# Softmax denominators from the third batch element on: VectorE turns and sums the exponentials in place of TensorE's multiplication by ones

## The chip, the cores and the metric

The kernel runs on one core of a Trainium2 chip. The metric is the time of one execution on the device in microseconds (us), lower is better. TensorE is written PE, VectorE DVE, ScalarE ACT, GpSimd POOL; SP is the engine whose queue issues most of the transfers.

## The reference

Eight batch elements, 12 heads, 448 positions, head size 64. Attention with normalised q and k, then a mixer over tokens (448 to 256 to 448) and over channels (768 to 1536 to 768), all in float32.

```python
q_n, k_n = rmsnorm(q, g_q), rmsnorm(k, g_k)            # (8, 12, 448, 64)
scores = matmul(q_n, k_n.T) / sqrt(64)
attn = exp(scores - max);  attn = attn / (sum(attn, over keys) + 1e-9)
x = matmul(attn, v)                                     # put together to (8, 448, 768)
h = max(x.T @ w_tok1, 0) @ w_tok2;   u = x + h.T
out = u + max(u @ w_ch1, 0) @ w_ch2
```

## The kernel before

Every instruction's place is set by the program: each engine runs its instructions in the order in which the code emits them (`manual_schedule`), and an instruction that waits holds up everything behind it on its engine. Lists of work items with costs are merged into one list (`merge`, `place`), and that order is the order on all engines.

Heads are taken in pairs `p` (0 to 47, six to a batch element) and pairs in steps of two, `t` (0 to 23, three to an element). While the mixer of element b runs, the attention of element b + 1 runs between its matmuls. The work of step t:

- `turn_qk`: from pair 12 on DVE turns q and k by 32x32 blocks (L436) and ACT scales q (L439).
- `score(t, k)` for seven groups k of 64 keys: four 64x64 matmuls (L459) make scores with keys on the partitions. They fill two of the four PSUM buffers of `ps_S`; ACT writes the exponentials (L463) to the tile `e`.
- `values`: four matmuls with v for each k add up the output (`o_ps`, L532).
- `group_sums(t, k)`: DVE adds the seven `e` tiles into `es` (L500). `es` is one buffer, 128x896: two pairs, 64 sums per head on the partitions.
- `row_sums(t)`: four matmuls with a matrix of ones (`one_c`, L512) add the 64 partitions of each head. The result `d_ps` takes the two other buffers of `ps_S`, and every partition of a head holds the denominator.
- `denominators`: for each pair DVE turns `d_ps` out of PSUM (`dt`, L561), takes reciprocals (`rc`, L563), turns them back spread over 32 columns (`rd`, L575) and multiplies `o_ps` into `uT` (L578).

From step t = 9 (`BIG`) a step is two blocks on PE: the first holds scores 0 and 1 of step t, the rest of `values` of step t - 1, `row_sums(t - 1)` and score 2; the second holds scores 3 to 6 and four of `values`. Six to eight units of the mixer stand between blocks (`BLOCKS`). Steps 6 to 8 are cut into four smaller parts by `att_step`.

The mixer's matmuls write `m_ps`, of which there are two buffers. In the first half of the channel mixer (`ch1`, L1102) a group of six matmuls fills one buffer, and DVE (L1108) or ACT (L1112, L1124) takes it out; seven such groups belong together (`PRODUCTS`, a form of Strassen's scheme). In the second half (`ch2`, L1168) eight matmuls fill a buffer, and DVE (L1183) or ACT (L1179) takes it out. X forms (L1142) are sums for ch2 on DVE and POOL.

Of the kernel before, what the change touches and what calls it, by code (L numbers as in the profile page):

```python
# [8 lines left out]
F32 = mybir.dt.float32  # L9
# [74 lines left out]
def whole(ctx, tc, shifted, pre, q, k, v, g_q, g_k, moe_w_tok1, moe_w_tok2, moe_w_ch1, moe_w_ch2, out):  # L84
# [454 lines left out]

    def row_sums(t):  # L540
        es = st.pop(("es", t))
        for p in (2 * t, 2 * t + 1):
            st["d", p] = s_tile("d_ps")
            ones(p, es[:, p % 2, :], start=True, stop=True)

    def denominators(ps):

        def begin(p):
            b, j = divmod(p, NPAIR)
            if j == 0:  # L550
                st["uT", b] = uT_pool.tile([P, NC, S], F32, name="uT")
# [9 lines left out]
            nc.vector.transpose(out=dt[:], in_=src)  # L561
            st["rc", p] = rc = pre.nt_pool.tile([P, NB], F32, name="rc")
            nc.vector.reciprocal(out=rc[:], in_=dt[:].rearrange("p (n c) -> p n c", c=32)[:, :, 0])  # L563

        def raw(p):

            b, j = divmod(p, NPAIR)
# [4 lines left out]
        def end(p):  # L572
            b, j = divmod(p, NPAIR)
            rd = rd_pool.tile([P, S], F32, name="rd", tag="rd")
            nc.vector.transpose(  # L575
                out=rd[:].rearrange("p (n c) -> p n c", c=32),
                in_=st.pop(("rc", p))[:].unsqueeze(2).to_broadcast([P, NB, 32]))
# [10 lines left out]
    def big_step(t, second):  # L588
# [6 lines left out]
        def first_block():  # L595
            if live:
                score(t, 0)
                score(t, 1)
            if more and t > BIG:
                pre.reduce(n, st)  # L600
                pre.square(n + 1, st)
            for k in range(NK - 2 - (t > BIG), NK):
                values(last, k)
            row_sums(t - 1)
            for i in last:
                st.pop(("v", i))
            if live:
                score(t, 2)
# [11 lines left out]
        if not second:  # L620
# [7 lines left out]
            between += roots[:1] + ends[:2] + roots[1:2]  # L628
            between += [it for both in zip(ends[2:], roots[2:4]) for it in both] if more else ends[2:]
# [5 lines left out]
        between += [item(group_sums, t, k) for k in (5, 6)] + loads(n + 3)  # L635
# [24 lines left out]
    def att_step(g):  # L660
# [8 lines left out]
        def finish():  # L669
# [7 lines left out]
            if s == 0 and t:  # L677
                if not on_pe(p - 1):
                    row_sums(t - 1)
# [72 lines left out]
        if live and not on_pe(p):  # L752
            items += [(0.5, lambda k=k: group_sums(t, k)) for k in ((), (1, 2), (3, 4), (5, 6))[s]]

# [13 lines left out]
        items += part(behind)  # L768
        if not inside and not soon:
# [580 lines left out]
    for b in range(B):  # L1350
# [24 lines left out]
        if b + AHEAD < B and (shifted or b < 2):  # L1375
# [18 lines left out]
        else:  # L1394
            if b + 1 < B:
                last = merge(last, x_items(b + 1, 1) + (behind_x if b == 1 and not shifted else []))
# [282 lines left out]
```

## Time and profile before

| | before |
|---|---|
| runs, us | 1268.9, 1271.52, 1271.26; median 1271.26 |
| span of the profiled execution, first to last instruction | 1265.4 us |
| busy PE, DVE, ACT, POOL | 1245.0, 830.5, 397.7, 441.6 us |
| granted TensorE clock | 1.000 |

The profiled execution's time is known only as its span; the three timed runs are 3.5 to 6.1 us longer than it, which is what lies around the first and the last instruction and the difference between executions. A row of the timeline gives the start, the duration, engine, line, operation, output and inputs, shape and count; in brackets how long the engine was idle before and what ended that. In the trace a float32 matmul is two records, so x8 is four matmuls. An m_ps group of ch1 is 12 records, one of ch2 16.

### The profile page before, as it was taken

Reading aid. Unit: us, or ns where it says so; the run is one execution under the profiler, and the core shown is the slowest. Engines: PE = TensorE matmul, PEld = TensorE weight load, DVE = VectorE, ACT = ScalarE, POOL = GpSimd, SP = SyncE. Lnnn points to the kernel's source line nnn. Section 1 sums busy time; section 2 is a strip of 40 time slices with the busy share of each in tenths; the row PEclk is TensorE's granted clock in tenths of the full one; section 3 lists DMA queues with packets and bytes.
Section 4 is the critical chain, followed back from the end, with each engine's and each line's share of the span. In section 5 each row is a group of like instructions: output and inputs, shape, how many; then the busy total and the mean of one; then the engine's idle time right before and its main releaser. Section 6 shows DMA issues by size and latency. Waiting matters only on the chain.

```text
span 1265.4 us, 20464 instructions
## 1 busy us (share of the span) xinstructions
PE 1245.0 (98%) x7340; PEld 906.1 (72%) x7340; DVE 830.5 (66%) x1307; ACT 397.7 (31%) x800; POOL 441.6 (35%) x681
## 2 busy tenths in 40 slices
PE   6999999999999999999999999999999999999998
PEld 3444444457744588788778877897787878798998
DVE  6989879756664455857677476766758486556243
ACT  5664443124231234403442144312343034301210
POOL 2311551044995912234224132234122242132222
PEclk9999999999999999999999999999999999999999
DMA  9566696899889786685758667684866855386554
GB/s 208 149 169 188 183 243 171 203 261 252 231 226 257 166 204 160 147 235 117 174 144 214 159 149 179 150 223 110 195 164 148 222 131 155 115 212 159 168 174 105
DMA packets 480274, 228.39 MB, mean 180 GB/s; under 512 B 362900, under 2 KB 440084, under 8 KB 480164
## 3 DMA queue, kind: packets, MB, share of 16 engines
q1 hardware_dynamic: 472626, 211.85, 67.2%
q0 software_dynamic: 4512, 14.46, 3.9%
q8 instruction: 60, 0.98, 0.3%
q10 hardware_dynamic: 3026, 0.69, 0.3%
q14 instruction: 50, 0.41, 0.1%
HBM read 184.26 MB, written 42.66 MB: 179 GB/s over the span
## 4 chain that ended last, share of the span: by engine, by line
PE 89%; DVE 4%; DMA 2%; SPq 1%; issue 1%; ACT 1%; DVEq 0%; ACTq 0%
PE m_ps L1102 25%; PE m_ps L1168 22%; PE s_ps L459 10%; PE o_ps L532 9%; PE m_ps L1072 5%; PE m_ps L1151 4%; PE m_ps L850 3%; PE t_ps L850 2%; PE m_ps L982 2%; PE seven_ps L936 2%; PE m_ps L936 1%; PE d_ps L512 1%; DMA v<-in_v_dram 1%; PE m_ps L512 1%; SPq L1517 1%
## 5 line engine op out<-in xcount | busy, mean ns | idle before, releaser
L1168 PEld LDWEIGHTS m_ps<-hb,unit 128*128 128x128 f32 x1440 | 271.0, 190 | 8.8 <-issue 7.7
L1168 PE MATMUL m_ps<-hb,unit 128*128 128x224 f32 x1440 | 277.2, 354 | 0.0
L1102 PE MATMUL m_ps<-tu,unit 128*128 128x224 f32 x1008 | 201.9, 355 | 0.6 <-ACT r L1112 0.4
L1102 PEld LDWEIGHTS m_ps<-tu,unit 128*128 128x128 f32 x1008 | 189.0, 190 | 14.7 <-issue 8.5
L463 ACT ACTIVATE e<-s_ps 128x448 f32<-128x448 f32 x294 | 138.4, 553 | 158.7 <-PE s_ps L459 158.3
L1102 PE MATMUL m_ps<-uT,unit 128*128 128x224 f32 x756 | 151.1, 354 | 0.0
L1102 PEld LDWEIGHTS m_ps<-uT,unit 128*128 128x128 f32 x756 | 142.2, 190 | 6.6 <-POOL tu L1006 2.8
L459 PE MATMUL s_ps<-qkT 64*64 64x448 f32 x1260 | 144.4, 545 | 1.2 <-ACT x L832 1.2
L532 PE MATMUL o_ps<-e,v 64*64 64x448 f32 x1148 | 130.5, 538 | 0.4 <-DMA v<-in_v_dram 0.3
L500 DVE TENSOR_TENSOR es<-es,e 128x896 f32<-128x896 f32 x90 | 102.0, 1133 | 12.5 <-ACT e L463 8.1
L1108 POOL TENSOR_TENSOR hb<-r,r 128x448 f32<-128x448 f32 x21 | 23.8, 1135 | 215.4 <-ACT r L1124 215.4
L1108 DVE TENSOR_TENSOR hb<-m_ps,r 128x448 f32<-128x448 f32 x63 | 39.0, 620 | 87.4 <-POOL r L1108 58.1
L459 PEld LDWEIGHTS s_ps<-qkT 64*64 64x64 f32 x1260 | 45.4, 132 | 69.0 <-issue 55.6
L532 PEld LDWEIGHTS o_ps<-e,v 64*64 64x64 f32 x1148 | 46.0, 133 | 63.7 <-issue 58.7
L1586 POOL TENSOR_TENSOR nt<-rs 128x56 f32<-128x56 f32 (+1 forms) x54 | 20.6, 381 | 197.1 <-DVE rs L1578 194.4
L1183 POOL TENSOR_TENSOR uT<-uT,r 128x448 f32<-128x448 f32 x42 | 51.4, 1239 | 78.3 <-DVE r L1183 46.7
L1109 ACT ACTIVATE hb<-hb 128x448 f32<-128x448 f32 x84 | 48.3, 576 | 90.2 <-DVE hb L1108 69.7
L1556 DVE TENSOR_REDUCE ms<-sq 128x28 f32<-128x896 f32 (+2 forms) x44 | 47.5, 1080 | 42.4 <-ACT sq L1543 35.7
L324 POOL TENSOR_TENSOR raw<-raw 128x128 f32<-128x128 f32 x128 | 66.2, 537 | 20.3 <-DMA raw<-wp 15.8
L1179 ACT COPY r<-m_ps 128x448 f32<-128x448 f32 x24 | 12.8, 532 | 156.6 <-PE m_ps L1168 156.6
L1183 DVE TENSOR_TENSOR uT<-uT,m_ps 128x448 f32<-128x448 f32 x41 | 24.9, 619 | 54.9 <-PE m_ps L1168 54.9
L1108 DVE TENSOR_TENSOR r<-m_ps,r 128x448 f32<-128x448 f32 x42 | 26.0, 618 | 50.8 <-PE m_ps L1102 50.8
(177 smaller groups left out, 1793.1 us busy)
## 6 DMA issues: line engine op xcount, KB each, us to landing
unit<-ws SPq DMA_DIRECT2D x267, 384.0 KB, 4.0
raw<-in_moe_w_ch_dram SPq DMA_DIRECT2D x72, 256.0 KB, 3.4
v<-in_v_dram SPq DMA_DIRECT2D x96, 112.0 KB, 3.8
out_dram<-turned SPq DMA_DIRECT2D x182, 56.0 KB, 2.0
xs<-xt SPq DMA_DIRECT2D x52, 168.0 KB, 4.4
qk_t<-in_q_dram SPq DMA_DIRECT2D x144, 56.0 KB, 3.6
qk_t<-in_k_dram SPq DMA_DIRECT2D x144, 56.0 KB, 3.6
x<-xs SPq DMA_DIRECT2D x39, 192.0 KB, 4.0
```

Of the source, the lines that this page charges most:

```text
L324: nc.gpsimd.tensor_tensor(out=at[o], in0=at[x], in1=at[y], op=ALU.add if op == "+" else ALU.subtract)
L459: nc.tensor.matmul(out=pss[i][rows_of(i, a), 0:S], lhsT=qkT[h, 1, k * D:(k + 1) * D], rhs=qkT[h, 0, :], start=True, stop=True)
L463: nc.scalar.activation(out=e[:, i, :], in_=pss[i][:, 0:S], func=AF.Exp)
L500: nc.vector.tensor_tensor(out=es[:], in0=(es if k > 1 else st["e", t, 0])[:], in1=st["e", t, k][:], op=ALU.add)
L532: nc.tensor.matmul(out=st["o", p][a * D:(a + 1) * D, 0:S], lhsT=vt[rows, k * D:(k + 1) * D], rhs=e[rows, :], **kw)
L850: nc.tensor.matmul(out=st["t1", h][jc][:, 0:HC], lhsT=w1_sb[:, c, jc * P:(jc + 1) * P], rhs=st["x", b, h][:, :, c, :], start=start and c = ...
L1072: nc.tensor.matmul(out=ps, lhsT=a[:, o + 2 * half, :], rhs=natural(half * KF + t) if wide else u[:, half * KC + t, :], start=(t == 0 and h ...
L1102: nc.tensor.matmul(out=ps[:, j * HS:(j + 1) * HS], lhsT=w[:, t, j, :], rhs=m, start=(t == 0), stop=(t == KC - 1))
L1108: add = lambda e, o, x, y: e.tensor_tensor(out=o, in0=x, in1=y, op=ALU.add)
L1151: nc.tensor.matmul(out=ps, lhsT=w[:, t, :], rhs=natural(half * KF + t), start=(half == 0 and t == 0), stop=(half == 1 and t == KF - 1))
L1168: nc.tensor.matmul(out=ps[:, x * HS:(x + 1) * HS], lhsT=st["w"][:, tile_at % 6, :], rhs=hb[:, X_SLOT[f], i, :], start=(i == 0), stop=(i == 3))
L1183: e.tensor_tensor(out=get(out), in0=get(x_), in1=get(y), op=ALU.add if op == "+" else ALU.subtract)
```

## The change

For pairs 12 and up (steps 6 to 23, 18 of them) the four matmuls with ones are no longer issued. DVE works on `es` itself instead: `add_keys` turns a pair's half of `es` by 32x32 blocks and sums 32 columns (the block's keys) by `tensor_reduce`. That gives the sum over 32 of a head's 64 partitions (`dn`); the other half lies 32 partitions away. `fold` has ACT copy it over in four pieces (`half`), `inverse` adds the two (three small additions on DVE, since the second pair's heads stand the other way round) and takes both pairs' reciprocals in one instruction. `dn`, `half` and `rc` live in the tile `v_first`, which holds the first pair's v and is free by then. `add_keys` and `fold` are emitted behind the last `group_sums` of the step; before, the turn and the reciprocals were emitted behind the first block of the next step. The last two steps of `denominators` stay.

Two smaller moves come with it. The roots of the next pairs' norms are started one place ahead of the first `rd`. For the third element's second half, the turn of x for the token mixer (`x_items(2, 1)`) moves ahead of the squares of step 10's q and k. The diff, without what only renames:

```diff
+    def ones_after(p):
+        return on_pe(p) or pre.plain(p)          # plain: p < 12
+
+    def key_sums(t):
+        p = 2 * t
+        few = pre.v_0[:, t % 2 * 6 * NB:(t % 2 + 1) * 6 * NB].rearrange("p (k i n) -> p k i n", k=3, i=2)
+        dn, half, rc = (few[:, k] for k in range(3))
+        def add_keys(i):
+            dt = rd_pool.tile([P, S], F32, name="dt", tag="rd")
+            nc.vector.transpose(out=dt[:], in_=st["es", t][:, i, :])
+            nc.vector.tensor_reduce(
+                out=dn[:, i, :], in_=dt[:].rearrange("p (n c) -> p n c", c=32), axis=AX_X, op=ALU.add)
+            if i:
+                st.pop(("es", t))
+        def fold():
+            for m in range(4):
+                nc.scalar.copy(out=half[32 * m:32 * m + 32], in_=dn[32 * (m ^ 1):32 * (m ^ 1) + 32])
+        def inverse():
+            whole = slice(0, P)
+            for i, rows, to in ((0, whole, whole), (1, slice(0, D), slice(D, P)), (1, slice(D, P), slice(0, D))):
+                nc.vector.tensor_tensor(out=rc[to, i, :], in0=dn[rows, i, :], in1=half[rows, i, :], op=ALU.add)
+            nc.vector.reciprocal(out=rc, in_=rc)
...
-        parts = [lambda p=p: begin(p) for p in ps]
+        parts = [lambda p=p: begin(p) for p in ps if ones_after(p)]
...
             for k in range(NK - 2 - (t > BIG), NK):
                 values(last, k)
-            row_sums(t - 1)
...
-            between += roots[:1] + ends[:2] + roots[1:2]
-            between += [it for both in zip(ends[2:], roots[2:4]) for it in both] if more else ends[2:]
+            between += roots[:2]
+            between += [it for both in zip(ends, roots[2:4]) for it in both] if more else ends
...
-        between += [item(group_sums, t, k) for k in (5, 6)] + loads(n + 3)
+        between += [item(group_sums, t, k) for k in (5, 6)] + [(0.4, fn) for fn in key_sums(t)[:2]] + loads(n + 3)
+        between += [(0.4, fn) for fn in key_sums(t)[2:]]
...
-                att = att[6:] + att_items(lo + 10, lo + per - 1) + ahead + [block] + beside + between[:-3]
+                att = att[6:] + att_items(lo + 10, lo + per - 1) + ahead + [block] + beside
+                att += between[:6] + x_items(2, 1) + between[6:-3]
```

What this does to the order on the engines. PE at the start of step 8, before (`v_71` and `v_69` are step 7's v, ch1 is the mixer):

```order
L532 MATMUL o_ps<-e,v_71 64x448 x2
L532 MATMUL o_ps<-e,v_69 64x448 x2
L459 MATMUL s_ps<-qkT 64x448 x4
L512 MATMUL d_ps<-es,one_c 64x448 x4
L1102 MATMUL m_ps<-tu,unit 128x224 x6
```

The same place after:

```order
L532 MATMUL o_ps<-e,v_71 64x448 x2
L532 MATMUL o_ps<-e,v_69 64x448 x2
L459 MATMUL s_ps<-qkT 64x448 x4
L1143 MATMUL m_ps<-tu,unit 128x224 x6
```

The four matmuls with ones are gone, at this and 17 other places, and no other row of PE's order in this half of the program has moved. DVE in step 7, from the last two turns of the next step's q and k to the reciprocals, before:

```order
L436 STREAM_TRANSPOSE qkT<-qk_t 128x448 x2
L500 TENSOR_TENSOR es<-es,e 128x896 x2
L1108 TENSOR_TENSOR hb<-m_ps,r_19924 128x448
L1108 TENSOR_TENSOR r_19982<-m_ps,r_19924 128x448
L1108 TENSOR_TENSOR r_19995<-m_ps,r_19982 128x448
L561 STREAM_TRANSPOSE dt<-d_ps 128x448
L563 RECIPROCAL rc<-dt 128x14
L561 STREAM_TRANSPOSE dt<-d_ps 128x448
L563 RECIPROCAL rc<-dt 128x14
```

And after:

```order
L436 STREAM_TRANSPOSE qkT<-qk_t 128x448 x2
L500 TENSOR_TENSOR es<-es,e 128x896 x2
L559 STREAM_TRANSPOSE dt<-es 128x448
L560 TENSOR_REDUCE v_first<-dt 128x14
L559 STREAM_TRANSPOSE dt<-es 128x448
L560 TENSOR_REDUCE v_first<-dt 128x14
L1149 TENSOR_TENSOR hb<-m_ps,r_19930 128x448
L1149 TENSOR_TENSOR r_19988<-m_ps,r_19930 128x448
L572 TENSOR_TENSOR v_first<-v_first 128x14
L572 TENSOR_TENSOR v_first<-v_first 64x14 x2
L573 RECIPROCAL v_first<-v_first 128x28
L1149 TENSOR_TENSOR r_20009<-m_ps,r_19988 128x448
```

Four long instructions now stand ahead of two that take m_ps out. ACT in an element's third step, between the q scaling and the exponentials of the next step's first scores, before:

```order
L439 ACTIVATE qkT<-qkT,g_t 128x448 x2
L1179 COPY r_21435<-m_ps 128x448
L1543 ACTIVATE sq<-qk_t 128x896
L1179 COPY r_21457<-m_ps 128x448
L463 ACTIVATE e<-s_ps 128x448 x4
```

And after:

```order
L439 ACTIVATE qkT<-qkT,g_t 128x448 x2
L1220 COPY r_21441<-m_ps 128x448
L567 COPY v_first<-v_first 32x28 x4
L1585 ACTIVATE sq<-qk_t 128x896
L1220 COPY r_21469<-m_ps 128x448
L463 ACTIVATE e<-s_ps 128x448 x4
```

The four copies wait for DVE's sums, with a square, a drain of m_ps and the exponentials behind them.

More of the change, by code (lines that the diff above doesn't have):

```diff
@@ L561, in begin, with home @@
             nc.vector.transpose(out=dt[:], in_=src)
-            st["rc", p] = rc = pre.nt_pool.tile([P, NB], F32, name="rc")
-            nc.vector.reciprocal(out=rc[:], in_=dt[:].rearrange("p (n c) -> p n c", c=32)[:, :, 0])
+            st["rc", p] = rc = pre.nt_pool.tile([P, NB], F32, name="rc")[:]
+            nc.vector.reciprocal(out=rc, in_=dt[:].rearrange("p (n c) -> p n c", c=32)[:, :, 0])
+        def home(p):
+            b, j = divmod(p, NPAIR)
+            if ("uT", b) not in st:
+                st["uT", b] = uT_pool.tile([P, NC, S], F32, name="uT")
         def raw(p):
+            home(p)
             b, j = divmod(p, NPAIR)
@@ L677, in finish @@
             if s == 0 and t:
-                if not on_pe(p - 1):
+                if not on_pe(p - 1) and ones_after(p - 1):
                     row_sums(t - 1)
@@ L753, in att_step @@
             items += [(0.5, lambda k=k: group_sums(t, k)) for k in ((), (1, 2), (3, 4), (5, 6))[s]]
+            adds = key_sums(t) if s == 3 and not ones_after(p) else []
+            items += part(adds[:2])
         if s == 0 and 5 < p + 1 < NP:
@@ L768, in att_step @@
         items += part(behind)
+        if live and not on_pe(p):
+            items += part(adds[2:])
         if not inside and not soon:
@@ L1395, in whole @@
             if b + 1 < B:
-                last = merge(last, x_items(b + 1, 1) + (behind_x if b == 1 and not shifted else []))
+                last = merge(last, behind_x if b == 1 and not shifted else x_items(b + 1, 1))
             if b == 2 and not shifted:
```

9 lines of the change are left out of this document (5 added, 4 removed).

## The prediction

> **What bounds the kernel now.** I read the page's busy shares and chain first, then who PE waited for, then the timeline at the places where the change acts.
>
> ```profile
> PE 1245.0 (98%) x7340; PEld 906.1 (72%) x7340; DVE 830.5 (66%) x1307; ACT 397.7 (31%) x800; POOL 441.6 (35%) x681
> PE 89%; DVE 4%; DMA 2%; SPq 1%; issue 1%; ACT 1%; DVEq 0%; ACTq 0%
> sum 150.00, PE 150.00 PEld 120.02 DVE 100.19 ACT 47.23 POOL 45.80; mean PE 10.00 PEld 8.00 DVE 6.68 ACT 3.15 POOL 3.05
> PE m_ps L1102 <- ACT r L1112: 0.4, 1, 0.4
> L512 PE MATMUL d_ps<-es,one_c x168: 535/536/537, 112.6 to 1117.2; 64*64 64x448 f32 x168
> ```
>
> PE is busy 98% of the span and makes up 89% of the chain. The third line is the sum of a table by stretches of 10 us from 600 to 750: PE never idle, DVE busy two thirds. In the list of PE's waits the only one for a drain of m_ps in ch1 is the 0.4 us shown. So PE's own work counts one for one, and DVE's counts only where it makes PE wait. The last line: 168 records of matmuls with ones are 21 steps of 8; 18 of these steps go.
>
> **What PE saves.** One such place, step 10's first block:
>
> ```profile
> 640.51 0.93 PE L532 MATMUL o_ps<-cv_sb,v 64*64 64x448 f32 x8
> 641.26 0.93 PE L512 MATMUL d_ps<-es,one_c 64*64 64x448 f32 x8
> 642.01 0.93 PE L459 MATMUL s_ps<-qkT 64*64 64x448 f32 x8
> ```
>
> From start to start the four matmuls take 0.75 us (642.01 - 641.26; the 0.93 contains a modelled end that overlaps the next). 18 x 0.75 = 13.5 us off PE, with no row of its order moved. `d_ps` also leaves `ps_S`, so score 2 takes the buffers of score 0 instead of those of score 1: it needs an exponential that ends 0.9 us earlier.
>
> **What DVE and ACT get.**
>
> ```profile
> L561 DVE STREAM_TRANSPOSE dt<-d_ps 128x448 f32<-128x448 f32 x42 | 25.9, 617 | 7.0 <-PE d_ps L512 7.0
> L563 DVE RECIPROCAL rc<-dt 128x14 f32<-128x14 f32 x48 | 11.6, 243 | 1.7
> L436 DVE STREAM_TRANSPOSE qkT<-qk_t 128x448 f32<-128x448 f32 x72 | 42.0, 618 | 1.3 <-PE s_ps L459 1.3
> L1556 DVE TENSOR_REDUCE ms<-sq 128x28 f32<-128x896 f32 x36 | 38.8, 1077 | 35.7 <-ACT sq L1543 35.7
> L1578 DVE TENSOR_SCALAR rs<-ms 128x56 int32<-128x56 int32 x18 | 3.8, 211 | 0.6
> L1564 ACT COPY half<-ms 32x56 f32<-32x56 f32 x72 | 16.9, 235 | 11.7 <-DVE ms L1556 10.3
> ```
>
> Per step DVE loses two turns out of PSUM and two reciprocals, 2 x (617 + 243) = 1.72 us (1.6 in sequence). It gets two turns out of SBUF at 618 ns and two sums over 448 columns, which the trace does not have; half of the sum over 896 is 540 ns. That is 2.3 us, with the dependences 2.4. Three additions at about 0.2 (from the 211 ns row) and a reciprocal over 28, between 0.24 and twice that, make 0.9. Net 2.4 + 0.9 - 1.6 = +1.7 us a step, 31 us in all, which takes DVE from 830 to about 861, or 68%. The page says nothing against that on the average. ACT gets four copies of at most 0.235 us a step, 0.9 us, 17 in all. The bounds for the new chain are 2.2 (half of each row, nothing for small ones) and 4.2 us (a 448-column sum as slow as the 1077 ns one).
>
> The load also moves: 3.3 us now lie behind the last `group_sums` and 1.6 fewer behind the next first block. The question is what is queued behind them. In DVE it is the drains of m_ps; in ACT, behind copies that wait for DVE, the exponentials, on which PE's score 2 waits. Three kinds of place are tight.
>
> **Step 7, ch1.**
>
> ```profile
> 325.45 4.81 PE L1102 MATMUL m_ps<-uT,unit 128*128 128x224 f32 x24
> 328.85 2.54 DVE L500 TENSOR_TENSOR es<-es,e 128x896 f32<-128x896 f32 x2 [0.48 <-ACT e L463]
> 330.02 0.55 ACT L1112 COPY r<-m_ps 128x448 f32<-128x448 f32 x1
> 330.62 4.81 PE L1102 MATMUL m_ps<-tu,unit 128*128 128x224 f32 x24 [0.36 <-ACT r L1112]
> 331.31 0.61 DVE L1108 TENSOR_TENSOR hb<-m_ps,r 128x448 f32<-128x448 f32 x1
> ```
>
> x24 are two groups of 2.4 us. The second group of the row at 325.45 is drained by DVE's L1108 at 331.31 to 331.9; the second group of the row at 330.62 needs that buffer at 333.0, 1.1 us later. In the new order the four long instructions stand ahead of that drain: es ends at 331.4, + 2.4 = 333.8, + 0.6 = 334.4. PE waits 1.4 us (0.9 to 2.5 by the bounds). All of it is shifted by what step 6 saves, DVE and PE alike, since DVE had waited for PE shortly before. POOL works there too:
>
> ```profile
> 317.10 1.06 DVE L1598 TENSOR_TENSOR nt<-nt,ms 128x56 f32<-128x56 f32 x1
> 279.72 0.22 DVE L1598 TENSOR_TENSOR nt<-nt,ms 128x56 f32<-128x56 f32 x1
> 316.95 1.14 POOL L1108 TENSOR_TENSOR hb<-r,r 128x448 f32<-128x448 f32 x1
> 312.69 1.08 DVE L1556 TENSOR_REDUCE ms<-sq 128x28 f32<-128x896 f32 x1
> 313.08 3.92 POOL L324 TENSOR_TENSOR raw<-raw 128x128 f32<-128x128 f32 x8 [15.80 <-DMA raw<-wp]
> ```
>
> The same small two-input addition takes 0.22 us alone and 1.06 us beside a POOL addition; the one-input sum keeps its 1.08 us while POOL works. So I leave the turns and sums, which have one input, at their price, and the three small additions can become slow. The Trainium skill, page "SBUF — State Buffer", section "SBUF: two separate sides", has this as an exclusive lock on a shared port pair: a GpSimd instruction and a VectorE instruction with two SBUF inputs shut each other out for their whole length, and a VectorE instruction with one input in its plain mode is not touched. By that rule the term stays 1.4 us; if instead every new instruction were stretched by a quarter it would be 2.0, and the sum below 10.2 in place of 10.8. The rows above agree with the rule.
>
> Steps 6 and 8 by contrast:
>
> ```profile
> 294.79 1.73 PE L532 MATMUL o_ps<-e,v 64*64 64x448 f32 x16
> 295.54 0.62 DVE L1108 TENSOR_TENSOR hb<-m_ps,r 128x448 f32<-128x448 f32 x1 [2.12 <-POOL r L1108]
> 382.85 1.34 DVE L500 TENSOR_TENSOR es<-e 128x896 f32<-128x896 f32 x1 [6.84 <-PE d_ps L512]
> ```
>
> In step 6 DVE waits 2.12 us ahead of the drain, which takes the new work in, and PE has turned to attention before it needs the buffer. Behind step 8's `es` DVE stands idle for 6.84 us. Neither costs.
>
> **An element's first step (9, 12, 15, 18, 21).**
>
> ```profile
> 743.51 2.21 DVE L500 TENSOR_TENSOR es<-es,e 128x896 f32<-128x896 f32 x2
> 747.41 1.73 PE L459 MATMUL s_ps<-qkT 64*64 64x448 f32 x16
> 748.27 0.95 ACT L1543 ACTIVATE sq<-qk_t 128x896 f32<-128x896 f32 x1 [2.49 <-DMA qk_t<-in_q_dram]
> 749.59 0.95 ACT L463 ACTIVATE cv_sb<-s_ps 128x448 f32<-128x448 f32 x2
> 751.22 0.93 PE L512 MATMUL d_ps<-es,one_c 64*64 64x448 f32 x8
> ...
> 600.49 1.73 PE L459 MATMUL s_ps<-qkT 64*64 64x448 f32 x16
> 601.50 0.98 ACT L463 ACTIVATE e<-s_ps 128x448 f32<-128x448 f32 x2 [0.75 <-PE s_ps L459]
> ```
>
> DVE's sums would end at 745.7 + 2.4 = 748.1, hidden in its idle time, since PE's next m_ps group is 5 us away. On ACT the copies stand between this square, a relu and the exponentials, so these start at about 750.7 in place of 749.6. Score 2, which now starts where `d_ps` did, at 751.22, needs the pair that ends at 751.6: 0.3 us of waiting. In the other four elements the square does not wait that long for its transfer; the last two rows are step 12, where the exponentials start 1.0 us behind the scores and not 2.2, and nothing is lost. Price 0.3 us, 0 to 2.
>
> **An element's third step, ch2 (11, 14, 17, 20, 23).**
>
> ```profile
> 520.79 0.62 DVE L1183 TENSOR_TENSOR uT<-uT,m_ps 128x448 f32<-128x448 f32 x1 [0.85 <-PE m_ps L1168]
> 523.22 1.09 DVE L500 TENSOR_TENSOR es<-es,e 128x896 f32<-128x896 f32 x1
> 527.40 0.62 DVE L1183 TENSOR_TENSOR r<-r,m_ps 128x448 f32<-128x448 f32 x1 [1.57 <-ACT r L1179]
> 531.80 1.08 DVE L1556 TENSOR_REDUCE ms<-sq 128x28 f32<-128x896 f32 x1 [1.06 <-ACT sq L1543]
> 532.15 14.17 PE L1168 MATMUL m_ps<-hb,unit 128*128 128x224 f32 x72
> 537.55 0.61 DVE L1183 TENSOR_TENSOR uT<-uT,m_ps 128x448 f32<-128x448 f32 x1
> ```
>
> DVE is nearly full here. The row at 532.15 holds 72 / 16 = 4.5 groups, 3.1 us each; the first group's buffer is wanted again by the third at 532.15 + 6.2 = 538.3, and DVE frees it at 538.2. The margin is 0.1 us. After, PE comes 0.75 us earlier. Ahead of that drain DVE has 3.3 us more and 1.6 us less, and waits 0.9 us for ACT's copies: +2.6. Against it stand its idle times of 1.57 and 1.06 in the rows, and 0.85 ahead of the drain that in the new order stands between the two `es`: 3.5. So DVE gains about 0.9, PE 0.75, and the margin stays near 0.2. A margin that thin breaks in some elements; I take 0.2 us each, 1.0 in all, between 0 (the gaps fill exactly) and 1.8 each (the long bound).
>
> By the same reckoning the second steps (10, 13, ...) keep a microsecond of room. SP's queue has the same transfers, shifted by a few rows around steps 8 and 9. The turn of x moved ahead only issues its transfers earlier, on POOL's queue, where two short root steps now stand behind them. The moved roots run where the turns of `d_ps` ran. These edits are put at nothing; their cover is the idle third of DVE and two thirds of POOL, and without it the late one would be the next q, a few tenths in one step.
>
> **The sum.** 13.5 - 1.4 - 0.3 - 1.0 = 10.8 us. The span goes from 1265.4 to 1254.6. The median of the runs shown, 1271.26, is 5.9 us above that span, and I carry this over: 1260.5 us.
>
> **Rivals.**
>
> - No place waits; the idle time of DVE takes everything. For it: PE's list of waits is almost empty. Against it: the drain in step 7, whose order I can read. 1271.26 - 13.5 = 1257.8.
> - DVE becomes the bound in ch2: the small additions of `inverse` are stretched by POOL from 0.22 to 1.06 us each, 2.5 us a step, and in an element's third step that lies ahead of the drain. It costs 5 x 2.5 = 12.5 in place of 1.0, so 13.5 - 1.4 - 0.3 - 12.5 = -0.7: 1272, no change. For it: the pair of rows at 279.72 and 317.10. Against it: the additions are a quarter as wide, and POOL is busy 3 in 10 of the time.
> - Slower: ACT becomes the bound. Copies that wait for DVE hold up the exponentials in every step, and score 2 waits with them. The point is a wait of (13.5 + 2.5) / 18 = 0.9 us a step. If each step lost 1.4 us as step 7 does, 25.2 - 13.5 = 11.7 more: 1283. Against it: ACT is busy 31% and the exponentials have over 1 us of room at most places.
>
> **How the numbers follow.** The bound for a difference is 0.2%, 2.5 us, about what a measurement of this kernel can tell. My forecast, 1258.5 to 1265, has 0.66; no waiting at all 0.18; no change 0.10; slower 0.06. Faster by over 2.5 us: the first two and a little of the third's lower edge, 0.86; within it 0.09; slower 0.05. The range reaches from the first rival less the 2 us by which the runs before differ, 1256, to a loss of 7 us in the third steps (five times 1.4), 1267.
>
> **What would show it.** PE's records of `d_ps` from 168 to 24, and its busy time down by about 13. A wait of PE for DVE's L1149 of over 1 us near 330. DVE busy about 860, sums of 128x14 near 0.55 us. Small waits of PE's L1209 for DVE's drains early in the ch2 run of each element. If sums take a full microsecond, or PE waits for ACT's exponentials in each step, I am wrong.

## The result, and the profile after

The changed kernel takes 1262.62 us (median of 5 runs, 1261.9 to 1263.57), the kernel before 1271.26 (median of 5, 1267.33 to 1272.57): the ratio is 0.9945, 95% interval 0.9929 to 0.9962. The change makes the kernel faster by 0.55%, 7 us by the ratio and 8.6 us by the medians. The profiled execution took 1262.04 us, with a span of 1260.2 us and a clock of 0.999. The lines of the page that answer to those of before:

```profile
PE 1234.3 (98%) x7196; PEld 900.9 (71%) x7196; DVE 867.8 (69%) x1379; ACT 412.2 (33%) x872; POOL 452.5 (36%) x681
PE 82%; DVE 7%; SPq 4%; DMA 3%; issue 2%; ACT 2%; DVEq 0%; ACTq 0%
L1209 PE MATMUL m_ps<-hb,unit 128*128 128x224 f32 x1440 | 277.0, 353 | 4.5 <-DVE uT L1224 4.5
```

PE's busy time fell by 10.7 us, DVE's grew by 37. PE's share of the chain fell from 89% to 82%, since the chain now runs through places where PE waits. In the groups by shape (busy us, mean ns) the matmuls with ones on `es` are down to 24, and the new work on DVE and ACT is:

```profile
L512 PE MATMUL d_ps<-es,one_c 64*64 64x448 f32 x24 | 2.8, 536 | 0.0
L559 DVE STREAM_TRANSPOSE dt<-es 128x448 f32<-128x448 f32 x36 | 23.0, 638 | 0.3
L560 DVE TENSOR_REDUCE v_first<-dt 128x14 f32<-128x448 f32 x36 | 22.3, 620 | 1.2
L572 DVE TENSOR_TENSOR v_first<-v_first 64x14 f32<-64x14 f32 x36 | 6.4, 177 | 0.8
L573 DVE RECIPROCAL v_first<-v_first 128x28 f32<-128x28 f32 x18 | 5.9, 328 | 0.6
L567 ACT COPY v_first<-v_first 32x28 f32<-32x28 f32 x72 | 15.3, 212 | 26.3 <-DVE v_first L560 25.1
```

A sum over 448 columns takes 620 ns, not 540. The list of PE's waits (us in total, times, longest) has three new entries for drains on DVE:

```profile
PE m_ps L1209 <- DVE uT L1224: 4.5, 4, 1.1
PE m_ps L1143 <- DVE hb L1149: 1.4, 1, 1.4
PE m_ps L1192 <- DVE uT L1197: 0.6, 1, 0.6
```

PE runs the same matmuls in the same order in both kernels, but for the 18 steps. So the time between the starts of the same two matmuls can be compared place by place. The table is worked out from PE's records in the traces; stretches are named by the clock of the changed kernel, and from the kernel before 0.75 us is taken off wherever a removed step lies in the stretch. So a stretch that holds a removed step and nothing else new comes out equal: from 353 to 406 us, with step 8's matmuls in it, both kernels have 52.94. Left out are the stretch up to 300 us, which differs between executions, and those in which the changed kernel and the kernel before agree to within 0.2 us.

| us between | 300-324 (step 6) | 324-334 (step 7, ch1) | 334-353 (7 to 8) | 406-417 | 417-460 | 500-545 (t=11) | 660-690 (14) | 810-836 (17) | 960-982 (20) |
|---|---|---|---|---|---|---|---|---|---|
| before | 24.08 | 9.15 | 17.45 | 10.09 | 43.18 | 44.06 | 28.72 | 24.83 | 21.04 |
| after | 24.08 | 11.31 | 17.35 | 10.95 | 43.18 | 45.14 | 29.80 | 25.90 | 22.10 |
| a0_again | 24.08 | 11.84 | 17.23 | 10.72 | 43.18 | 45.13 | 29.81 | 25.91 | 22.11 |
| e1_no_key_sums | 27.23 | 10.38 | 20.03 | 10.09 | 43.18 | 43.93 | 28.58 | 24.69 | 21.26 |
| e2_x_later | 24.08 | 11.72 | 18.50 | 10.35 | 43.18 | 46.48 | 32.60 | 27.24 | 23.48 |
| e3_sums_behind_drains | 24.08 | 10.33 | 19.16 | 10.98 | 43.18 | 45.14 | 29.80 | 25.91 | 22.11 |
| e4_second_square_tile | 24.08 | 11.60 | 17.18 | 11.10 | 43.33 | 45.15 | 28.64 | 24.74 | 20.93 |
| e5_x_move_undone | 24.08 | 11.01 | 18.56 | 10.09 | 49.45 | 45.14 | 29.79 | 25.90 | 22.10 |
| e6_fold_on_vector | 24.08 | 11.57 | 18.51 | 10.80 | 43.18 | 44.97 | 29.62 | 25.74 | 21.96 |
| e8_loads_ahead | 24.08 | 11.54 | 18.27 | 10.09 | 43.18 | 45.14 | 29.80 | 25.92 | 22.11 |
| g1_all_repairs | 24.08 | 11.31 | 23.10 | 10.09 | 43.28 | 43.98 | 28.64 | 24.75 | 20.95 |
| g2_sums_behind_v_by_scalar | 24.22 | 12.87 | 22.02 | 10.27 | 43.17 | 45.14 | 29.80 | 25.91 | 22.10 |
| g3_no_key_sums_v_by_scalar | 24.36 | 14.15 | 17.13 | 15.23 | 43.28 | 43.93 | 28.58 | 24.69 | 20.91 |
| g4_square_tile_and_loads | 24.29 | 11.62 | 21.21 | 10.09 | 43.28 | 43.99 | 28.65 | 24.75 | 20.94 |

So 13.5 us are won in 18 equal pieces: wherever nothing else changes, taking off 0.75 us a step leaves a difference of at most 0.2 us. Lost are 1.07 us in each third step 11, 14, 17 and 20 (4.3), 2.2 in step 7 and 0.9 near 407. Another 1.3 was lost ahead of 262 us, where the change does nothing.

### The profile page after: what moved, and what is told of

It is laid out like the page before. It is cut to its first block, busy times and chain, and to the rows that moved or that the text cites. A ratio compares the mean times of both kernels' runs of the same rounds, so it can differ in the third digit from the quotient of the medians.

```text
span 1260.2 us, 20320 instructions
## 1 busy us (share of the span) xinstructions
PE 1234.3 (98%) x7196; PEld 900.9 (71%) x7196; DVE 867.8 (69%) x1379; ACT 412.2 (33%) x872; POOL 452.5 (36%) x681
## 4 chain that ended last, share of the span: by engine, by line
PE 82%; DVE 7%; SPq 4%; DMA 3%; issue 2%; ACT 2%; DVEq 0%; ACTq 0%
PE m_ps L1143 26%; PE m_ps L1209 18%; PE s_ps L459 9%; PE o_ps L532 9%; PE m_ps L1113 5%; PE m_ps L891 3%; PE t_ps L891 2%; PE m_ps L1192 2%; PE m_ps L1023 2%; PE seven_ps L977 2%; DMA qk_t<-in_k_dram 2%; PE m_ps L977 1%; SPq L1563 1%; DVE es L500 1%; SPq L412 1%
## 5 line engine op out<-in xcount | busy, mean ns | idle before, releaser
L1209 PE MATMUL m_ps<-hb,unit 128*128 128x224 f32 x1440 | 277.0, 353 | 4.5 <-DVE uT L1224 4.5
L1209 PEld LDWEIGHTS m_ps<-hb,unit 128*128 128x128 f32 x1440 | 271.3, 190 | 12.8 <-issue 7.1
L500 DVE TENSOR_TENSOR es<-es,e 128x896 f32<-128x896 f32 x90 | 106.1, 1179 | 13.8 <-ACT e L463 9.4
L1149 POOL TENSOR_TENSOR hb<-r,r 128x448 f32<-128x448 f32 x21 | 23.9, 1140 | 218.6 <-ACT r L1165 218.6
L1224 POOL TENSOR_TENSOR uT<-uT,r 128x448 f32<-128x448 f32 x42 | 54.6, 1315 | 86.6 <-DVE r L1224 49.6
L1149 DVE TENSOR_TENSOR hb<-m_ps,r 128x448 f32<-128x448 f32 x63 | 38.8, 618 | 64.9 <-POOL r L1149 45.0
L1598 DVE TENSOR_REDUCE ms<-sq 128x28 f32<-128x896 f32 (+2 forms) x44 | 47.0, 1069 | 48.4 <-ACT sq L1585 41.4
L1113 PE MATMUL m_ps<-hb,stage 128*128 128x448 f32 x144 | 57.1, 556 | 2.0 <-ACT r L1124 1.9
```

Of the source, the lines that this page charges most:

```text
L500: nc.vector.tensor_tensor(out=es[:], in0=(es if k > 1 else st["e", t, 0])[:], in1=st["e", t, k][:], op=ALU.add)
L1113: nc.tensor.matmul(out=ps, lhsT=a[:, o + 2 * half, :], rhs=natural(half * KF + t) if wide else u[:, half * KC + t, :], start=(t == 0 and h ...
L1149: add = lambda e, o, x, y: e.tensor_tensor(out=o, in0=x, in1=y, op=ALU.add)
L1209: nc.tensor.matmul(out=ps[:, x * HS:(x + 1) * HS], lhsT=st["w"][:, tile_at % 6, :], rhs=hb[:, X_SLOT[f], i, :], start=(i == 0), stop=(i == 3))
L1224: e.tensor_tensor(out=get(out), in0=get(x_), in1=get(y), op=ALU.add if op == "+" else ALU.subtract)
```

## The experiments

Theory: DVE's program order makes drains of m_ps late at three kinds of place (the third steps, step 7, near 407), each by a cause of its own, and nothing else of the change costs time. Rivals: the sheer amount of DVE's work, ACT's copies, the moved x, the transfers. The runs follow in the order of the table and are called by the first part of their label (a0, e1 to e8, g1 to g4; there is no e7). Where an edit adds or removes lines, the numbers behind it shift in that run's rows: L1142 is L1149, L1211 is L1209, L1590 is L1585, L1603 is L1598.

### The changed kernel once more

> The changed kernel once more. The alignment of the two profiles gives 13.5 us won on TensorE and 8.3 us of waiting: about 5.1 in the third steps 11, 14, 17, 20 (1.3 each, VectorE's drain L1224), 2.1 in step 7, 0.8 near 406 us (drain L1197), and 1.0 net near 205 to 215 us, where that profile shows a clock of 0.5 to 0.65. Theory: the first three are set by the order of instructions and come again to within 0.1 us; the one at 205 is a matter of that execution and may be gone, and the span is then 1259.2 to 1260.2. Rival: the waits are scatter between executions; then they come at other places or sizes. Time 1261 to 1264, ratio 0.993 to 0.996.

1261.48 us, ratio 0.994 (0.992 to 0.996), span 1259.5. The third steps came again to within 0.02 us. Step 7 lost 2.7 where it had lost 2.2, and the stretch near 407 0.6 for 0.9, so these two do vary between executions, by more than the 0.1 expected. The loss ahead of 262 us was gone (0.0). The waits belong to the order of instructions, that one loss to its execution.

### The key sums left out

```diff
         def add_keys(i):
-            dt = rd_pool.tile([P, S], F32, name="dt", tag="rd")
...
         def fold():
-            for m in range(4):
-                nc.scalar.copy(out=half[32 * m:32 * m + 32], in_=dn[32 * (m ^ 1):32 * (m ^ 1) + 32])
+            pass
         def inverse():
-            whole = slice(0, P)
...
```

> Leaves out the sums, copies, additions and reciprocals that give the denominators of pairs 12 and up; all else, with the moved roots and the moved turn of x, stays as in the changed kernel. It prices TensorE's saving with nothing in its place. Theory: only the new work on VectorE and ScalarE holds TensorE up. The waits of L1209 and L1149 for DVE go (5.1 + 1.5 to 2.1), the wait near 406 us stays, since there DVE waits for a late square: span 1252.5 to 1254, time 1254 to 1257, ratio to before about 0.988. Rival: the moved roots, x or transfers, or TensorE's buffers, cost the 5 us; then the span stays at 1257 or more and the time over 1259.5.

1259.67 us, ratio 0.992 (0.9894 to 0.9946), span 1257.5: a miss by some 4 us, at the numbers of the rival. In ch2 the theory held, 43.93 and 28.58 are even 0.1 below the kernel before. But PE now waits for v in steps 6 to 8 (timeline of this run):

```profile
307.58 1.24 PE L532 MATMUL o_ps<-e,v 64*64 64x448 f32 x4 [1.93 <-DMA v<-in_v_dram]
352.17 1.54 PE L532 MATMUL o_ps<-e,v 64*64 64x448 f32 x4 [2.32 <-DMA v<-in_v_dram]
```

From 300 to 417 us this run needs 121.05 us, the changed kernel 117.0 and the kernel before 114.1 (115.6 less two steps). So the rival is right in part: in this stretch it is transfers that take the gain. Without the key sums step 7 is 0.9 us shorter and the wait near 407 is gone, though the theory had it stay, but the waits for v take more than that. Step 7 still stands 1.2 above the kernel before (10.38 to 9.15), with none of the new work in it.

### The turns of x moved behind the first block

```diff
-            blocks[4][3].extend(x_items(b + 1, 0))
+            blocks[5][3][8:8] = x_items(b + 1, 0)
```

> In ch2 the four turns of x for the element's first half stand behind the next step's first block instead of ahead of the drains that follow the key sums; nothing is left out. Theory: DVE's drain L1224 is late only because a fixed run of DVE work (sums, square's two reductions, x turns) stands ahead of it; with 2.5 us of turns moved behind, the four waits of 1.1 us are gone and TensorE gains 5.1 us less what the moved turns cost: span 1255 to 1256, time 1257 to 1259. Rival (DVE is full in ch2 whatever the order): the wait comes at a later drain instead, and the time stays within 1 us of the changed kernel, 1262.

1269.87 us, ratio 0.9999 (0.9978 to 1.0019): a miss, and in the wrong direction. The waits in ch2 grew from 1.1 to 2.2 us. The timeline at the first of them:

```profile
526.81 2.68 POOL L1224 TENSOR_TENSOR uT<-uT,r 128x448 f32<-128x448 f32 x2 [6.42 <-DVE r L1224]
527.31 2.39 DVE L572 TENSOR_TENSOR v_first<-v_first 128x14 f32<-128x14 f32 x3
536.36 0.62 DVE L615 TENSOR_TENSOR uT<-o_ps,rd 128x448 f32<-128x448 f32 x1
537.90 0.61 DVE L1224 TENSOR_TENSOR uT<-uT,m_ps 128x448 f32<-128x448 f32 x1
```

With the turns gone, the three small additions of `inverse` fell beside POOL's two additions and took 2.39 us in place of 0.54 (row at 527.06 below), and a `rd` with its product, 1.3 us, moved ahead of the drain, since the list is spread by the number of its items. So the edit took 1.6 us from ahead of the drain and put more there. It cannot decide between the theory and its rival; it shows the second rival of the prediction at work, though not in the changed kernel, whose three additions took 0.54 at this place. The longest single addition is 1115 ns here and 366 ns there. The Trainium skill, page "SBUF — State Buffer", section "SBUF: two separate sides", has a VectorE instruction with two SBUF inputs and a GpSimd instruction that reads SBUF shut each other out; the rows agree.

### Steps 6 to 8 with the sums behind the drains

```diff
             adds = key_sums(t) if s == 3 and not ones_after(p) else []
-            items += part(adds[:2])
+            pass
...
-            items += part(adds[2:])
+            items += part(adds)
```

> In steps 6 to 8 the turns and sums for the denominators stand behind the drains of ch1 (and with the small additions), not ahead; nothing is left out. Theory: step 7's wait of 1.4 us for DVE's L1149 goes, with the 0.4 to 0.5 around it: -1.4 to -2.0 us, span 1258.2 to 1258.8, and the ch2 waits stay at 1.1 each. Rival (the wait comes from the exponentials or POOL's share of the drains): TensorE waits as long at the same place, and the time does not move.

1261.13 us, ratio 0.9936 (0.9916 to 0.9956), span 1258.4. Step 7's stretch fell by 1.0 to 10.33, and the wait of 1.4 us is gone, as forecast; the 0.4 to 0.5 around it stayed. Rows of DVE and PE in the changed kernel:

```profile
334.75 0.61 DVE L1149 TENSOR_TENSOR hb<-m_ps,r 128x448 f32<-128x448 f32 x1
335.42 2.54 PE L1143 MATMUL m_ps<-tu,unit 128*128 128x224 f32 x12 [1.36 <-DVE hb L1149]
```

And in this run, with POOL's row first:

```profile
313.93 3.84 POOL L324 TENSOR_TENSOR raw<-raw 128x128 f32<-128x128 f32 x8 [17.98 <-DMA raw<-wp]
321.69 0.62 DVE L1149 TENSOR_TENSOR hb<-m_ps,r 128x448 f32<-128x448 f32 x1 [1.03 <-POOL r L1149]
330.12 0.61 DVE L1149 TENSOR_TENSOR hb<-m_ps,r 128x448 f32<-128x448 f32 x1
347.80 1.44 PE L532 MATMUL o_ps<-e,v 64*64 64x448 f32 x4 [1.54 <-DMA v<-in_v_dram]
```

The drain at 330.12 stands at 334.75 in the changed kernel; of the 4.6 us between them 2.4 are the lead that this execution had already at 324 us. The stretch is still 1.2 us above the kernel before. DVE's drain at 321.69 waited 1.03 us for POOL's addition, which stood behind POOL's wait of 17.98 us for weights; e1 has the same 1.03. So 1.2 us are lost at this place even where the key sums don't stand ahead of its drains. The next stretch gave back 1.8, since PE then waited for v. That the span lies within the forecast is luck: it is 1.8 below the changed kernel's because of that lead of 2.4.

### A second tile for the squares

```diff
+            if b == 3:
+                pre.sq_b = raw_tile()[:].rearrange("p n w -> p (n w)").bitcast(F32)
...
-            sq = self.sq[:].rearrange("p r d -> p (r d)")[:, 0:n * d].rearrange("p (r d) -> p r d", d=d)
+            flat = self.sq[:].rearrange("p r d -> p (r d)")
+            if p % 2 and getattr(self, "sq_b", None) is not None:
+                flat = self.sq_b
+            sq = flat[:, 0:n * d].rearrange("p (r d) -> p r d", d=d)
```

> From the fourth element on the odd pair's squares go to a second tile, so that ScalarE need not wait for VectorE's reduction of the even pair's before it writes them; all else as in the changed kernel. It reaches the third steps 14, 17 and 20, not 11. Theory: the 1.06 us that DVE waits between the two reductions (and which the prediction counted as room) is a chain reduction, square, reduction; with a second tile the square runs ahead, DVE's drain comes about 1 us earlier, and the waits of TensorE at 14, 17, 20 fall from 1.1 to 0.1 or 0.2: 3 us, span about 1257. That at 11 stays at 1.1. Rival (the sheer amount of DVE's work, or ScalarE's copies, makes the drain late): the waits stay at 1.0 or more.

1258.55 us, ratio 0.9902 (0.9868 to 0.9935), span 1256.2. This is the clearest hit. At 14, 17 and 20 the whole loss is gone (28.64, 24.74, 20.93, at or below the kernel before), and at 11, which the tile does not reach, it stays (45.15). The changed kernel at step 11, then this run at step 14 (rows of ACT, DVE and PE):

```profile
523.57 0.65 DVE L559 STREAM_TRANSPOSE dt<-es 128x448 f32<-128x448 f32 x1
527.06 0.54 DVE L572 TENSOR_TENSOR v_first<-v_first 128x14 f32<-128x14 f32 x3 [0.99 <-ACT v_first L567]
531.62 1.04 DVE L1598 TENSOR_REDUCE ms<-sq 128x28 f32<-128x896 f32 x1
532.75 0.95 ACT L1585 ACTIVATE sq<-qk_t 128x896 f32<-128x896 f32 x1 [2.58 <-issue]
533.73 1.08 DVE L1598 TENSOR_REDUCE ms<-sq 128x28 f32<-128x896 f32 x1 [1.06 <-ACT sq L1585]
538.27 0.61 DVE L1224 TENSOR_TENSOR uT<-uT,m_ps 128x448 f32<-128x448 f32 x1
539.03 21.24 PE L1209 MATMUL m_ps<-hb,unit 128*128 128x224 f32 x111 [1.13 <-DVE uT L1224]
```

```profile
675.05 0.98 ACT L1590 ACTIVATE raw<-qk_t 128x896 f32<-128x896 f32 x1
676.68 1.05 DVE L1603 TENSOR_REDUCE ms<-sq 128x28 f32<-128x896 f32 x1
677.64 1.07 DVE L1603 TENSOR_REDUCE ms<-raw 128x28 f32<-128x896 f32 x1
682.18 0.61 DVE L1224 TENSOR_TENSOR uT<-uT,m_ps 128x448 f32<-128x448 f32 x1
676.64 13.54 PE L1209 MATMUL m_ps<-hb,unit 128*128 128x224 f32 x69
```

In the first fence the square starts where the first reduction has ended, at 532.7, though ACT stood free for 2.58 us: both squares use one tile. The 1.06 us of DVE are a chain, reduction, square, reduction, that moves with the work ahead of it. In the second fence the square ran 1.6 us before the first reduction, the reductions follow each other, and PE does not stop. DVE does the same work, so its amount alone was not the cause: either less work (e1) or the second tile takes the wait away.

### The move of x undone

```diff
-                att += between[:6] + x_items(2, 1) + between[6:-3]
+                att += between[:-3]
...
-                last = merge(last, behind_x if b == 1 and not shifted else x_items(b + 1, 1))
+                last = merge(last, x_items(b + 1, 1) + (behind_x if b == 1 and not shifted else []))
```

> The turn of x for the third element's second half is put back to where it was in the kernel before; the key sums stay. Theory: the move is worth nothing, since it only issues transfers earlier: within 0.8 us of the changed kernel, waits in ch2 and at step 7 as there. Rival: the move is part of the gain (the tokens' mixer waits for x without it): 2 us or more slower, with a wait of TensorE near 450 to 480 us.

1264.92 us, but from 1259.01 to 1269.59; ratio 0.9933 (0.9906 to 0.996). By the times it can't be told from the changed kernel. The profiled execution (span 1267.8) shows a wait for x such as the rival named, though near 425 and not 450 to 480 us. Its timeline and its table of windows (PE, PEld, DVE, ACT and POOL busy, then PEclk, share of DMA, GB/s):

```profile
424.91 3.07 PE L898 MATMUL t_ps<-x,w_sb 64*128 64x384 f32 x4 [1.95 <-DMA x<-xs]
```

```profile
420.00:422.00 2.00, 2.00 (x7) 0.95 (x5) 0.00 (x0) 0.00 (x0) 1.83 (x5) 1.00 0.97 222
426.00:428.00 2.00, 2.00 (x4) 0.59 (x3) 0.00 (x0) 0.00 (x0) 1.92 (x5) 0.50 0.81 125
428.00:430.00 2.00, 2.00 (x4) 1.09 (x5) 0.00 (x0) 0.00 (x0) 1.84 (x6) 0.50 0.17 26
432.00:434.00 2.00, 2.00 (x8) 1.19 (x7) 0.00 (x0) 0.49 (x2) 1.90 (x4) 1.00 0.90 254
```

PE waited 1.95 us for x, and the granted clock was 0.50 for some 6 us after it: 6.3 us lost in 417-460. The kernel before has the turn of x in the same place, and its one trace has no such wait (43.18). So the move seems to buy room for a transfer that is late in some executions only; how often is not known.

### The copies on DVE in place of ACT

```diff
-                nc.scalar.copy(out=half[32 * m:32 * m + 32], in_=dn[32 * (m ^ 1):32 * (m ^ 1) + 32])
+                nc.vector.tensor_copy(out=half[32 * m:32 * m + 32], in_=dn[32 * (m ^ 1):32 * (m ^ 1) + 32])
```

> The four small copies between partitions run on VectorE instead of ScalarE. Theory: VectorE then has 0.7 to 0.8 us more a step but no longer waits 1.0 us for ScalarE; the ch2 waits of TensorE change by -0.2 each, and the time by less than 1 us; step 7's wait stays or grows by 0.5. Rival (ScalarE's copies, standing behind its exponentials and drains, are what makes the drain late): the four waits of 1.1 us fall below 0.4 and the time falls by 3 us or more.

1262.66 us, ratio 0.9939 (0.991 to 0.9968). The third steps lose 0.14 to 0.18 less each, as forecast. ACT's copies are not what makes the drain late.

### Pair 21's loads ahead of the sums

```diff
+            if t == BIG - 1 and s > 2:
+                items += part(pre.loads(n + s, st, nc.sync, nc.sync), 0.3)
             items += part(adds[:2])
...
-        if t == BIG - 1 and s > 1 and not shifted:
+        if t == BIG - 1 and s == 2 and not shifted:
```

> In step 8 the loads of pair 21's q and k are emitted ahead of the key sums, so that SP's queue has them ahead of the loads of x again, as in the kernel before; all else as in the changed kernel. Theory: the key sums' places in the list moved these loads behind five transfers of x, the square of k waited 17 us for them and held a reduction and the drain L1197 behind it; put back, the wait of 0.6 us near 406 goes: -0.8 us, span about 1259.4, less than the timed runs can tell. Rival: the transfer is late for another cause (traffic of the weights), and TensorE waits at 406 as before.

1260.67 us, ratio 0.9914 (0.9884 to 0.9944), span 1260.5. That is 1.1 above the forecast, since this execution lost some 2 us in its first 20, where the change does nothing. The wait near 407 is gone: 10.09, as before. In the changed kernel it had come about so (SP's queue, ACT, PE):

```profile
381.72 6.25 SPq L1563 DMA_DIRECT2D qk_t<-in_q_dram  x3
388.91 1.45 SPq L849 DMA_DIRECT2D x<-xs  x3
394.41 6.88 SPq L1563 DMA_DIRECT2D qk_t<-in_k_dram  x4
403.42 0.95 ACT L1585 ACTIVATE sq<-qk_t 128x896 f32<-128x896 f32 x1 [17.12 <-DMA qk_t<-in_k_dram]
407.60 1.77 PE L1192 MATMUL m_ps<-hb,unit 128*128 128x448 f32 x4 [0.59 <-DVE uT L1197]
```

Since the key sums have costs in the list, the loads of k were emitted behind x and went out at 394.41. In the kernel before they had gone out at 387.67, ahead of x:

```profile
387.67 2.04 SPq L1521 DMA_DIRECT2D qk_t<-in_k_dram  x4
```

The square waited for them, a reduction for the square, and the drain stood behind the reduction. The 0.8 us are too few for the times; the trace shows them.

### v from ScalarE's queue, and all repairs together

The next three runs issue the v of pairs 15 and 17 from ACT; the first has all repairs (the square tile from `b == 2` on), the second only the sums behind the drains, the third no key sums.

```diff
                 finish()
+                if s == 0 and p + 1 in (15, 17):
+                    load_v(p + 1, nc.scalar)
...
-        if s == 0 and 5 < p + 1 < NP:
+        if s == 0 and 5 < p + 1 < NP and (shifted or p + 1 not in (15, 17)):
```

> The changed kernel with four repairs: the second square tile, from the third element on (so that it reaches steps 11, 14, 17 and 20); steps 6 to 8 with the key sums behind the drains; pair 21's loads ahead of the key sums; the v of pairs 15 and 17 issued from ScalarE's queue straight behind the exponentials of the step's first part. Theory (each wait has its own cause and they add): 4 x 1.15 in ch2, 1.5 in step 7 that is no longer lost to v near 349 us, 0.8 near 407: 6.9 us off the changed kernel's span, 1253 to 1254, time about 1255, ratio to before 0.987 to 0.990. Rival (a wait taken away comes back at the next place): 1256.5 or more, with new entries in TensorE's list of waits.

> The run with the sums behind the drains, and the v of pairs 15 and 17 issued from ScalarE's queue, ahead of SP's loads of q and k. Theory: what that run won in step 7 (1.5 us) it lost again near 349 us, where TensorE waited 1.5 us for v, since the v of pair 17 stands in SP's queue behind loads of q, k and weights that wait; with v ahead, TensorE's wait for v is gone there and the 2.0 us lost at 349 stay won: span about 1256.5. Rival (v is late because the transfers themselves are slow then): the wait stays above 1 us and the span at 1258.

> The run without key sums (denominators of pairs 12 and up left out), with the v of pairs 15 and 17 issued from ScalarE's queue. Theory: that run lost 2.4 us near 307 and 2.8 near 349 to v alone; with v early it shows TensorE's whole saving, and the span falls from 1257.5 to 1252 to 1253, 12.5 to 13.5 us below the kernel before. Rival (something else in the rest of the change holds TensorE): 1256 or more.

1259.92, 1264.81 and 1260.21 us; ratios 0.9923 (0.9903 to 0.9944), 0.996 (0.9944 to 0.9977) and 0.9938 (0.9918 to 0.9958). All three missed. For the first and the third the rival's numbers came out (spans of 1261.2 and 1262.6). The span of the second, 1266.0, lies above both its theory and its rival. In ch2 the first won what it should (43.98, 28.64, 24.75, 20.95: 4.6 us less than the changed kernel). But 300 to 417 us took 122.7, 122.7 and 124.2 us, against 117.0. The second run, from its timeline, and the time from issue to landing of that v:

```profile
343.09 1.30 ACTq L412 DMA_DIRECT2D v<-in_v_dram  x2
352.81 0.56 PE L532 MATMUL o_ps<-e,v 64*64 64x448 f32 x1 [1.81 <-DMA v<-in_v_dram]
```

```profile
DMA to landing us min/median/max: 10.4/10.4/10.4
```

In the changed kernel the same load is issued at 342.89 by SP, lands 6.3 us later (in e3, from SP too, 7.9), and the DMA engines are full then (table of windows):

```profile
340.00:345.00 5.00, 5.00 (x30) 4.69 (x26) 1.46 (x3) 1.51 (x3) 4.47 (x10) 1.00 0.98 274
345.00:350.00 5.00, 5.00 (x36) 3.12 (x35) 1.43 (x3) 2.30 (x4) 4.84 (x9) 1.00 1.22 280
```

So my theory that v was late because it stood behind other loads in SP's queue is wrong, and the rival has the cause: from another queue v took no less from issue to landing, since the transfers themselves take longer. The Trainium skill, page "DMA: Bandwidth & Descriptors", section "Issuing engines are not separate DMA queues", says that loads issued by different engines share the same DMA engines; the 10.4 us agree. The third run shows how the same stretch holds the other engines:

```profile
319.39 5.07 POOL L324 TENSOR_TENSOR raw<-raw 128x128 f32<-128x128 f32 x8 [22.61 <-DMA raw<-wp]
326.66 0.62 DVE L1142 TENSOR_TENSOR hb<-m_ps,r 128x448 f32<-128x448 f32 x1 [5.35 <-POOL r L1142]
```

POOL's sums of weights wait for their transfer (319.4, in the changed kernel 313.95), the mixer's additions on POOL stand behind them, and DVE's drain behind those; PE waited 2.9 us. Near 407 this run lost another 5.1 (15.23), since the square of k waited 20.03 us for its transfer, the case of e8 again.

### The two repairs that worked

```diff
+            if b == 2:
+                pre.sq_b = raw_tile()[:].rearrange("p n w -> p (n w)").bitcast(F32)
...
+            if t == BIG - 1 and s > 2:
+                items += part(pre.loads(n + s, st, nc.sync, nc.sync), 0.3)
```

> The changed kernel with the two repairs that worked: the second square tile from the third element on, and pair 21's loads ahead of the key sums; steps 6 to 8 and the transfers there are left as in the changed kernel, since three runs lost at 307 to 353 us what they won there. Theory: 4 x 1.15 in ch2 and 0.8 near 407 come off the changed kernel, whose span was 1259.5 and 1260.2: 1254 to 1255.5, time 1256 to 1258, ratio to before 0.988 to 0.991; TensorE's list of waits has no L1209 of over 0.3 us. Rival (a wait taken away comes back at the next place): span 1258 or more.

1257.64 us (1254.58 to 1258.56), ratio to before 0.9891 (0.9868 to 0.9914). The time is as forecast, while the span, 1256.8, lies above the theory's 1255.5 and below the rival's 1258. It is the fastest version of the study, faster than the kernel before by 1.1%, and its interval lies below both intervals of the changed kernel (0.9929 to 0.9962 and 0.992 to 0.996). All five repaired places are at their values of before, and the group of ch2's matmuls stands without idle time:

```profile
L1211 PE MATMUL m_ps<-hb,unit 128*128 128x224 f32 x1440 | 276.9, 353 | 0.0
```

Its profiled execution, 1258.56 us, was its slowest and took 3.9 us more than the changed kernel in 334-353, with the transfers' order there unchanged.

## Why the prediction was right, and where it was wrong

Right were the sign, the mechanism (PE's own work counts one for one, and is lost where DVE's drains come late) and the range. The time came out 2.1 us above the forecast. That it came so close is partly luck, for two errors of opposite sign stand behind it. The span was 1260.2 us and not 1254.6; and the 5.9 us that I added to it were in fact 2.4 (1262.62 - 1260.2). In later runs of the kernel before, span and time differ by 2.1 us, as in 1267.9 us with a span of 1265.8; so its profiled execution took some 1267.5, 3.8 below the median. That part is a difference between executions of the kernel before, and the changed kernel has less of it (its profiled execution lies 0.6 below its median). Where a usual execution of the kernel before loses these us stays open: there is one trace of it, of a quick execution. The granted clock gives a hint: of the 24 later executions measured beside a0, the five at a clock of 0.997 took 1273.2 to 1275.9 us, the other 19, at 0.998 to 1.000, 1265.9 to 1271.2.

The terms in us, from the table and the two profiles of the changed kernel:

| term | predicted | after | again |
|---|---|---|---|
| 18 steps of four matmuls | -13.5 | -13.5 | -13.5 |
| step 7, ch1 | +1.4 | +2.2 | +2.7 |
| first steps (9, 12, ...) | +0.3 | 0 | 0 |
| third steps (11, 14, ...) | +1.0 | +4.3 | +4.3 |
| near 407 | 0 | +0.9 | +0.6 |
| ahead of 262 us, no change there | 0 | +1.3 | 0.0 |
| rest | 0 | -0.3 | 0.0 |
| sum | -10.8 | -5.1 | -5.9 |

- **PE's saving** came as forecast: 0.75 us a step leaves at most 0.2 us over wherever a removed step is the only change. At the other places it can't be seen by itself.
- **Step 7**: the named wait came out at 1.36 us where 1.4 was forecast. Around it PE lost 0.4 more at ACT's L1153 and 0.2 to 0.5 at the drain ahead. Two things the term missed. About 1.2 us are lost here even with no key sums ahead of the drains (e1, e3), where DVE's drain waits for POOL and POOL for weights. And winning this place wins nothing: with the wait put right (e3), the time goes to v 13 us later. The lower bound of 0.9 does not follow from the 2.2 us given for the new chain (331.4 + 2.2 + 0.6 - 333.0 is 1.2).
- **Third steps**: this is the step that failed. I set +2.6 us of work against 1.57 + 1.06 + 0.85 us of idle time. The 1.06 was no room but the chain through the one square tile (e4 removed it, and with it the whole loss), a sum was 80 ns longer than estimated, 0.16 us a step, and two root steps of the norms, put at nothing, moved ahead of the drain and took 0.35 us more (rows below: the first of them stood behind the drain of 537.55 in the kernel before and stands ahead of the drain of 538.27 in the changed one). The size, 1.07, lies inside the bounds that I gave, 0 to 1.8. In step 23 nothing was lost.

```profile
538.08 0.21 DVE L1573 SCALAR_TENSOR_TENSOR ms<-ms,half 128x56 f32<-128x56 f32 x1
536.92 0.21 DVE L1615 SCALAR_TENSOR_TENSOR ms<-ms,half 128x56 f32<-128x56 f32 x1
```

- **First steps**: ACT's copies did stand ahead of the exponentials, and PE lost nothing; the term could have been left out.
- **Edits at nothing**: the loads moved behind x cost 0.6 to 0.9 us (e8), though I had seen that they shift; I had named the next q, and it was the next k. The move of x is not free of effect either: without it 6.3 us were lost in the one execution traced.
- **Busy times**: DVE 868 where 861 was forecast; ACT +14.5 for 17; PE -10.7 for -13, and -12.0 in the second profile, where the mean clock was 1.000.
- **Rivals**: no addition of `inverse` took over 366 ns in the changed kernel; against it e2's row shows that the three together cost 1.85 us more as soon as their place in time moves. ACT never became the bound.

## What to carry to other kernels

Before idle time of an engine is counted as room for new work, look at what ends it: if its releaser itself waits for this engine (one buffer, written and read in turn), the gap moves along with the work and absorbs nothing. In a stretch in which the DMA engines are full (a busy share near 1 at 340 to 350 us) a wait removed came back here at the next transfer, and issuing the late load from another engine's queue did not help. An edit that only moves items in a list spread by number or cost also moves the loads behind them: compare the queue of transfers as well as the engines.

## What the hardware showed

A wait of PE of about 2 us can cost two or three times its length. 1.95 us (e5) were followed by some 6 us at a granted clock of 0.50, 6.3 us lost in all; 2.00 us in g4 by 0.50 at 352 to 354, 3.9 lost in all; 1.89 us in the changed kernel, near 212, by 0.50 at 214 to 216. Not each is: e1's 2.32 us were followed by full clock, as its table of windows has it, of e2's four waits of 2.2 us in ch2 only that near 686 lowered the clock, and none of the 1.1 us waits in ch2 did.

```profile
352.00:354.00 2.00, 1.83 (x5) 0.67 (x6) 1.83 (x2) 2.00 (x6) 1.84 (x4) 1.00 0.88 233
```

The Trainium skill, page "TensorE: Matmul & The Clock Gate", section "Why this matters for your kernels", puts the gap that lowers the clock at over about 3 us; here one of 1.95 did. The same page, section "What's actually happening", has the clock follow a window of activity that runs free of the kernel's start; that would explain that only some gaps do, but no run here shows the window.
